# Hourglass attention and a gated FFN on one core: from pair 14 on, two head pairs share a stretch of scores and a stretch of outputs

## The chip, the cores and the metric

The kernel runs on one NeuronCore of a Trainium2 chip. The metric is the time of one execution in microseconds (us), as the device takes it; lower is better. The engines are named as in the profile: PE (TensorE, matrix products), PEld (its weight loads), DVE (VectorE), ACT (ScalarE), POOL (GpSimd) and SP (SyncE, which here issues DMAs only). Each works through its own instructions in order and waits for others by semaphores.

## What is computed

Attention over q, k, v of shape 8 x 8 x 576 x 64 (batch, head, position, width) in two parts that are added, and then a feed-forward network over the result:

```python
q_d, k_d, v_d = (t.reshape(B, H, 144, 4, D).mean(axis=3) for t in (q, k, v))
out_d = sm_attn(q_d, k_d, v_d)                    # softmax over all 144 pooled positions
out_up = np.repeat(out_d, 4, axis=2)
mask = np.abs(pos[:, None] - pos[None, :]) < 4    # a band of 7 keys a query
out_local = softmax(where(mask, scale * q @ k.T, -1e9)) @ v
x = (out_up + out_local).transpose(0, 2, 1, 3).reshape(4608, 512)
out = (np.maximum(x @ w_gate, 0) * (x @ w_val)) @ w_out   # 512 -> 1536 -> 512
```

## The kernel before, in words

**Attention** goes by pairs of heads: 32 pairs, pair `p` being heads 2p and 2p+1, four pairs to a batch. Per pair there are a pooled part (144 x 144 scores a head) and a local part (24 groups of 24 queries, each against 32 keys). On TensorE a pair needs five kinds of product: `pooled_v` (L352, v averaged over four positions), `pooled_out` (L367), `pooled_scores` (L382), `local_scores` (L407, 48 small ones) and `local_out` (L424, 48 small ones). Each kind addresses the array in tiles of its own shape, the profile's 128*32, 64*72, 64*32 and 32*64. Their results lie in two PSUM tensors of two banks each, `ata` and `atb`, at the column offsets `U, SCO, OD, VD1 = 0, 144, 336, 432` (L344). The other four banks, `fpsum`, rotate among the FFN's results.

**The other engines' part of a pair** is:

- ACT: `cast_q` and half of `cast_k` (L235, to fp16), `pooled_bias` (L447), four `pooled_exp` (L475), `local_exp` (L485), and the copies out of PSUM `evict_vd` (L489, L491) and `evict_od` (L546).
- DVE: `pooled_max` (L437), `add_mask` (L452), `local_max` (L460), the other half of `cast_k` (L237), `add_x` (L557, two instructions, adds both parts into `xT`), `pooled_recip` (L498), `local_sum` (L528, L529), `turn_local` (L540).
- POOL: `local_sub` (L463), `pool_q` and `pool_k` (L320 to L333, the sums over four positions of q and k into the tile `pd`, which `pooled_scores` reads), `pooled_weights` (L502), `local_weights` (L532), `cast_v` (L239).
- SP: the loads of q, k and v, the stores of y, and two DMAs that transpose: `turn_dma` (L314, casted q and k into `qkT`, from pair 11 on) and `turn_pooled` (L507, the pooled weights into `adT`).

**The FFN** goes by units in a fixed list. An `h` unit is 8 products of 512 columns (L573, the two halves of 128 hidden rows for 512 tokens), a relu on ACT (L582) and a product on DVE (L585, called the gate below); a `y` unit is 12 products (L598) and a copy on ACT (L607). A chunk of 512 tokens is 12 `h` and 4 `y` units. Its first `h` unit reads `xT` rows of four pairs, one pair for each of the four accumulated products.

**The order** of all instructions is that of the source; nothing reorders them. Pairs 0 to 8 and the first 11 FFN units go by the hand-written list `ORDER`. Then comes a loop over steps `s` from 9 to 33, which this change is about. A step starts the scores of pair `s` and the outputs of pair `s - 2` in one stretch on TensorE, and then puts one FFN unit at a time between the pieces of the other engines' work (L720 to L777). In each step from 14 on the four units are `h`, `y`, `h`, `h`. `store_y` issues the stores of finished y. After the loop 33 units of FFN alone are left.

Small tiles rotate by pair number: `pd` and `qkT` by 3, `vw`, `vd16`, `pT`, `adT` and `st32` by 4, `vst` by 3, `qk16`, `e_d`, `col`, `sm`, `dd`, `ee`, `pp`, `odx` by 2.

Of the kernel before, what the change touches and what calls it, by code (L numbers as in the profile page):

```python
# [14 lines left out]
AX = mybir.AxisListType  # L15

N_PE = 11
NEG = -1.0e9


# [73 lines left out]
def kernel(  # L94
# [201 lines left out]
    def flat(p):  # L296
        return qkT[p % 3].rearrange("p j t -> p (j t)")
# [43 lines left out]

    U, SCO, OD, VD1 = 0, 144, 336, 432  # L344

    def pooled_v(p, part=(0, 1)):
        for n in range(6):
            x = n % 4
            if n // 4 not in part:
                continue  # L350
            for h in range(2) if n >= 4 else (None,):
                nc.tensor.matmul(  # L352
                    out=atb[32 * x : 32 * x + 32, 1, OD : OD + 128]
                    if h is None
                    else ata[32 * x : 32 * x + 32, h, VD1 : VD1 + 64],
                    lhsT=p32,
                    rhs=vw[p % 4][:, :, n, :] if h is None else vw[p % 4][:, h, n, :],
                    start=True,
                    stop=True,
                    tile_position=(0, 32 * x),  # L360
                )

    def pooled_out(p):
        vd, ad = vd16[p % 4], adT[p % 4]
        for kc in range(2):
            for x in range(4):
                nc.tensor.matmul(  # L367
                    out=atb[32 * x : 32 * x + 32, 0, OD : OD + SD],
                    lhsT=vd[:, kc, 32 * x : 32 * x + 32],
                    rhs=ad[:, x // 2, :, kc, 0:72],  # L370
                    start=(kc == 0),
                    stop=(kc == 1),
                    tile_position=(0, 32 * x),
                    skip_group_check=True,
                )

    def pooled_scores(p):
        pdt = pd[p % 3]
        for c in range(2):
            for h in range(2):  # L380
                lo = 64 * h
                nc.tensor.matmul(  # L382
                    out=ata[0:72, h, SCO + SD * c : SCO + SD * c + SD],
                    lhsT=pdt[lo : lo + 64, c, 0, :],
                    rhs=pdt[lo : lo + 64, :, 1, :],
                    start=True,
                    stop=True,
                    tile_position=(lo, 0),
                )

    def local_scores(p):
        qt, kt = flat(p), k_view(qkT[p % 3])
        for n in range(6):
            for g in range(4):
                c, m = n // 3, 4 * (n % 3) + g
                b = 24 * (4 * n + g)
                for h in range(2):
                    lo = 64 * h
                    if p < N_PE:
                        queries = qt[lo : lo + 64, b + 584 * c : b + 584 * c + 32]  # L400
                        keys = qt[lo : lo + 64, S // 2 + b : S // 2 + b + 32]
                    else:
                        queries = qt[lo : lo + 64, b : b + 32]
                        keys = kt[lo : lo + 64, c, :, 6 * m : 6 * m + 8].rearrange(
                            "p r g -> p g r"
                        )
                    nc.tensor.matmul(  # L407
                        out=atb[32 * g : 32 * g + 32, h, SCO + 32 * n : SCO + 32 * n + 32],
                        lhsT=queries,
                        rhs=keys,  # L410
                        start=True,
                        stop=True,
                        tile_position=(lo, 32 * g),
                    )

    def scores(p):
        pooled_scores(p)
        local_scores(p)

    def local_out(p):  # L420
        for n in range(6):
            for h in range(2):
                for g in range(4):
                    nc.tensor.matmul(  # L424
                        out=(ata, atb)[g // 2][64 * h : 64 * h + 64, g % 2, U + 24 * n : U + 24 * n + 24],
                        lhsT=vw[p % 4][32 * g : 32 * g + 32, h, n, :],
                        rhs=pT[p % 4][32 * g : 32 * g + 32, 6 * h + n, 0:24],
                        start=True,
                        stop=True,
                        tile_position=(32 * g, 64 * h),  # L430
                    )
# [2 lines left out]

    def pooled_max(p):
        c = col[p % 2]
        nc.vector.tensor_reduce(  # L437
            out=c[0:72, 36:40].rearrange("p (h c) -> p h c", h=2),
            in_=ata[0:72, :, SCO : SCO + 2 * SD].rearrange("p h (c j) -> p h c j", c=2),
            axis=AX.X,  # L440
            op=ALU.max,
            negate=True,
        )
# [5 lines left out]
        )  # L449

    def add_mask(p):
        nc.vector.tensor_tensor(  # L452
            out=sm[p % 2].rearrange("p (h n) j -> p h (n j)", h=2),
            in0=atb[:, :, SCO : SCO + 192],
            in1=_sap(mask, (0, 128), 0, [[0, 2], [1, 192]]),
            op=ALU.add,
        )
# [11 lines left out]

    def pooled_exp(p, h):  # L470
        c = col[p % 2]
        for cc in range(2):
            hc = 2 * h + cc
            lo = SCO + SD * cc
            nc.scalar.activation(  # L475
                out=e_d[p % 2][0:72, h, cc, 0:6, 0:24],
                in_=ata[0:72, h, lo : lo + SD].rearrange("p (n j) -> p n j", j=24),
                func=AF.Exp,
                bias=c[0:72, 40 + hc : 41 + hc],
                scale=scale / 16.0,  # L480
                accum_out=c[0:72, 44 + hc : 45 + hc],
            )
# [3 lines left out]

    def evict_vd(p, kc):
        if kc == 0:
            nc.scalar.copy(out=vd16[p % 4][:, 0, :], in_=atb[:, 1, OD : OD + 128])  # L489
        else:  # L490
            nc.scalar.copy(  # L491
                out=vd16[p % 4][0:64, 1, :].rearrange("p (h d) -> p h d", h=2),
                in_=ata[0:64, :, VD1 : VD1 + 64],
            )

    def pooled_recip(p):
# [47 lines left out]
    def evict_od(p):  # L544

        nc.scalar.copy(  # L546
            out=odx[p % 2].rearrange("p (g n m) -> p g n m", g=4, n=6),
            in_=atb[:, 0, OD : OD + SD].rearrange("p (n g m) -> p g n m", g=4, n=6),
        )

    def add_x(p, half=(1, 0)):
        b, kk = p // 4, p % 4
        x = xT[:, kk, b * S : (b + 1) * S].rearrange(
            "p (n g m f) -> p g n m f", n=6, g=4, f=4
        )
        for i in half:
            nc.vector.tensor_tensor(  # L557
                out=x[:, 2 * i : 2 * i + 2],
                in0=(ata, atb)[i][:, :, U : U + SD].rearrange(
                    "p g (n m f) -> p g n m f", n=6, f=4  # L560
                ),
                in1=_sap(odx[p % 2], (0, 128), 72 * i, [[36, 2], [6, 6], [1, 6], [0, 4]]),
                op=ALU.add,
            )
# [152 lines left out]
        stages[stage](int(number), *engine)  # L717
    pos[0] = ORDER.count("ga:")

    for s in range(9, NP + 2):  # L720
        now, nxt, two = s < NP, s + 1 < NP, s + 2 < NP
        if s + 3 < NP:
            load_qk(s + 3)
            load_v(s + 3)
        store_y()
        if now:
            pooled_v(s)
        pooled_out(s - 2)
        if now:
            scores(s)  # L730
        local_out(s - 2)
        evict_od(s - 2)
        if nxt:
            cast_v(s + 1, "pool")
        if now:
            evict_vd(s, 0)
            pooled_max(s)
            add_mask(s)
            local_max(s)
            local_sub(s)  # L740
        if two:
            cast_q(s + 2, "act")
        ffn(1)
        if now:
            pooled_bias(s)
            pooled_exp(s, 0)
            pooled_exp(s, 1)
        if two:
            cast_k(s + 2, 0, "dve")
        add_x(s - 2)  # L750
        if nxt and s + 1 >= N_PE:
            pool_q(s + 1)
            pool_k(s + 1)
        if now:
            local_exp(s)
            evict_vd(s, 1)
            pooled_recip(s)
            pooled_weights(s)
            local_sum(s)
            local_weights(s)  # L760
        ffn(1)
        if two:
            cast_k(s + 2, 1, "act")
            turn_dma(s + 2)
        if now:
            turn_pooled(s)
        if s + 1 < N_PE:
            turn_pe(s + 1)
            evict_half(s + 1, 0, None, "act")
# [2 lines left out]
            evict_half(s + 1, 1, 1, "dve")  # L772
            evict_sums(s + 1, 1, "dve")
        ffn(1)
        if now:
            turn_local(s)
        ffn(1)  # L777
    while pos[0] < len(units):
        ffn(1)
        store_y()  # L780
# [30 lines left out]
```

## Time and profile before

| what | us |
|---|---|
| runs of the kernel | 383.83, 388.38, 388.03; median 388.03 |
| the profiled execution | 384.85 |
| its span, first to last instruction | 383.1 |
| PE busy / DVE / ACT / POOL in the span | 362.6 / 217.0 / 214.2 / 183.1 |
| one step of the loop at 210 to 220 us | 9.50 |

In the rows of the timeline the first number is the start in us from the span's start, the second how long it took; x counts instructions merged into the row, and in brackets stand idle time ahead of it and what ended it. An instruction of DVE, ACT or POOL can start some hundredths before the record of the one ahead of it ends, so what an instruction costs its engine is read from start to start. A PE row's length holds the time to pass the array, so TensorE too is read from start to start.

### The profile page before, as it was taken

To read this page: it belongs to the slowest core of one execution; us is meant where nothing else is said; L and a number is where in the kernel's file an instruction comes from. 1 tells how busy PE (TensorE), PEld (TensorE's weight loads), DVE (VectorE), ACT (ScalarE), POOL (GpSimd) and SP (SyncE) were. 2 spreads that over 40 slices of the span, in tenths; PEclk is the share of its full clock that TensorE was granted. 3 is DMA by queue.
4 is the path that set the end of the run, shared out by engine and by line. 5 is a ranking of instruction groups with operands and counts; after the bars stand their busy time and mean duration, and the time that the engine had idled before them with its cause. 6 is when DMAs were issued, how large, how long until landed. Compare 5 with 4: busy or idle time off the path is not lost.

```text
span 383.1 us, 13146 instructions
## 1 busy us (share of the span) xinstructions
PE 362.6 (95%) x5476; PEld 186.1 (49%) x5476; DVE 217.0 (57%) x456; ACT 214.2 (56%) x644; POOL 183.1 (48%) x242
## 2 busy tenths in 40 slices
PE   2877997899999999999999999999999999999996
PEld 2756543454554444455545554555554444444442
DVE  2766785566666666666666666666666232222220
ACT  3868685366666666666666666666655322333231
POOL 5788785435666666666666666666652000000000
PEclk9955699899999999999999999999999999999999
DMA  7998999968889999999999999995842000100012
GB/s 263 257 239 247 193 205 207 207 115 173 191 189 190 190 190 193 185 196 182 200 190 187 194 174 202 197 190 119 153 68 70 29 29 29 55 27 29 27 40 99
DMA packets 140920, 58.63 MB, mean 153 GB/s; under 512 B 121852, under 2 KB 133308, under 8 KB 140860
## 3 DMA queue, kind: packets, MB, share of 16 engines
q1 hardware_dynamic: 135660, 52.93, 65.7%
q0 software_dynamic: 4768, 4.72, 7.7%
q8 instruction: 43, 0.70, 0.8%
q10 hardware_dynamic: 432, 0.14, 0.2%
q14 instruction: 17, 0.14, 0.1%
HBM read 42.05 MB, written 9.44 MB: 134 GB/s over the span
## 4 chain that ended last, share of the span: by engine, by line
PE 85%; DMA 5%; POOL 3%; SPq 2%; issue 2%; DVE 1%; ACT 1%; POOLq 0%; ACTq 0%; DVEq 0%
PE h_ps L573 47%; PE y_ps L598 24%; DMA vst<-in_v_dram 5%; PE atb L407 3%; PE ata L424 3%; PE ata L382 2%; PE t_ps L286 2%; PE atb L424 1%; SPq L177 1%; PE atb L367 1%; PE atb L352 1%; PE t_ps L280 1%; SPq L218 1%; POOL dd L463 1%; POOL qk L239 1%
## 5 line engine op out<-in xcount | busy, mean ns | idle before, releaser
L585 DVE TENSOR_TENSOR gT<-r,h_ps 128x512 f16<-128x512 f16 x108 | 74.0, 686 | 97.4 <-PE h_ps L573 92.6
L573 PE MATMUL h_ps<-xT,wg 128*128 128x512 f16 x432 | 113.2, 386 | 0.0
L573 PE MATMUL h_ps<-xT,wv 128*128 128x512 f16 x432 | 111.1, 381 | 0.0
L598 PE MATMUL y_ps<-wo,gT 128*128 128x512 f16 x432 | 98.6, 379 | 0.0
L582 ACT ACTIVATE r<-h_ps 128x512 f16<-128x512 f32 x108 | 64.3, 597 | 49.9 <-PE h_ps L573 49.8
L463 POOL TENSOR_TENSOR dd<-sm,col 128x384 f32<-128x384 f32 x32 | 26.6, 832 | 86.0 <-DVE col L460 86.0
L598 PEld LDWEIGHTS <-gT 128*128 128x128 f16 x432 | 42.3, 98 | 50.9
L573 PEld LDWEIGHTS <-wv 128*128 128x128 f16 x432 | 42.1, 98 | 50.7 <-issue 1.1
L573 PEld LDWEIGHTS <-wg 128*128 128x128 f16 x432 | 39.9, 99 | 45.3 <-issue 2.0
L475 ACT ACTIVATE e_d<-ata,col 72x144 f16<-72x144 f32 x128 | 46.7, 370 | 1.4 <-PE ata L352 0.2
L607 ACT COPY y_sb<-y_ps 128x512 f32<-128x512 f32 x36 | 21.1, 586 | 40.0 <-PE y_ps L598 39.8
L502 POOL TENSOR_TENSOR e_d<-e_d,col 72x576 f16<-72x576 f16 x32 | 36.6, 1144 | 4.8 <-DVE col L498 3.5
L437 DVE TENSOR_REDUCE col<-ata 72x4 f32<-72x576 f32 x32 | 24.1, 753 | 23.5 <-PE atb L424 21.2
L546 ACT CAST odx<-atb 128x144 f16<-128x144 f32 x32 | 8.9, 279 | 49.5 <-PE atb L424 47.6
L235 ACT CAST qk<-st 96x768 f16<-96x768 f32 (+3 forms) x45 | 33.5, 745 | 1.6 <-DMA st<-in_k_dram 1.6
L239 POOL CAST vw<-vst 128x768 f16<-128x768 f32 x32 | 26.3, 823 | 7.9 <-DMA vst<-in_v_dram 5.0
L532 POOL TENSOR_TENSOR pp<-ee,col 128x384 f16<-128x384 f16 x32 | 26.5, 831 | 0.0
L475 ACT ACTIVATION_READ_ACCUMULATOR e_d<-ata,col 72x1 f32 x128 | 24.9, 194 | 0.0
L540 DVE STREAM_TRANSPOSE pT<-pp 128x384 f16<-128x384 f16 x32 | 18.3, 573 | 9.2 <-POOL pp L532 9.1
L424 PE MATMUL atb<-pT,vw 32*64 32x24 f16 x768 | 18.7, 190 | 1.8 <-issue 1.8
L452 DVE TENSOR_TENSOR sm<-atb,mask 128x384 f32<-128x384 f32 x32 | 17.5, 545 | 2.8 <-POOL vw L239 1.0
L407 PE MATMUL atb<-qkT 64*32 64x32 f16 x1536 | 18.3, 211 | 0.7 <-issue 0.7
(52 smaller groups left out, 378.0 us busy)
## 6 DMA issues: line engine op xcount, KB each, us to landing
vst<-in_v_dram SPq DMA_DIRECT2D x126, 96.0 KB, 4.7
st<-in_q_dram SPq DMA_DIRECT2D x32, 288.0 KB, 4.8
out_dram<-y_sb SPq DMA_DIRECT2D x36, 256.0 KB, 3.3
st<-in_k_dram SPq DMA_DIRECT2D x20, 320.0 KB, 6.0
st<-in_k_dram SPq DMA_DIRECT2D x11, 288.0 KB, 5.0
wo<-in_moe_w_out_dram POOLq DMA_DIRECT2D x4, 384.0 KB, 7.8
wg<-in_moe_w_gate_dram POOLq DMA_DIRECT2D x2, 384.0 KB, 6.5
wv<-in_moe_w_val_dram POOLq DMA_DIRECT2D x2, 384.0 KB, 7.3
```

Of the source, the lines that this page charges most:

```text
L235: nc.scalar.copy(out=out, in_=in_)
L239: nc.gpsimd.tensor_copy(out=out, in_=in_)
L407: nc.tensor.matmul(out=atb[32 * g : 32 * g + 32, h, SCO + 32 * n : SCO + 32 * n + 32], lhsT=queries, rhs=keys, start=True, stop=True, tile ...
L424: nc.tensor.matmul(out=(ata, atb)[g // 2][64 * h : 64 * h + 64, g % 2, U + 24 * n : U + 24 * n + 24], lhsT=vw[p % 4][32 * g : 32 * g + 32, ...
L463: nc.gpsimd.tensor_tensor(out=dd[p % 2], in0=sm[p % 2], in1=_sap(col[p % 2], (0, 128), 0, [[1, 12], [0, 32]]), op=ALU.subtract,)
L475: nc.scalar.activation(out=e_d[p % 2][0:72, h, cc, 0:6, 0:24], in_=ata[0:72, h, lo : lo + SD].rearrange("p (n j) -> p n j", j=24), func=AF ...
L502: nc.gpsimd.tensor_tensor(out=ed, in0=ed, in1=_sap(col[p % 2], (0, 72), 48, [[1, 4], [0, 6], [0, 24]]), op=ALU.mult)
L532: nc.gpsimd.tensor_tensor(out=pp[p % 2], in0=ee[p % 2], in1=_sap(col[p % 2], (0, 128), 24, [[1, 12], [0, 32]]), op=ALU.mult,)
L573: nc.tensor.matmul(out=ps, lhsT=(wg, wv)[i][:, kk, 128 * j : 128 * j + 128], rhs=xT[:, kk, TCH * c : TCH * c + TCH], start=(kk == 0), stop ...
L582: nc.scalar.activation(out=r1[j % 3], in_=h_ps[c, j, 0], func=AF.Relu)
L585: nc.vector.tensor_tensor(out=gT[c % 2][:, j, :], in0=r1[j % 3], in1=h_ps[c, j, 1], op=ALU.mult)
L598: nc.tensor.matmul(out=ps, lhsT=gT[c % 2][:, j, 128 * t : 128 * t + 128], rhs=wo[:, j, :], start=(j == 0), stop=(j == NJ - 1),)
```

## The change

Steps 9 to 13 stay single steps. From pair 14 (`TWO`) on, one pass of a loop handles an even pair `e` and the odd pair `o = e + 1`. It has two stretches on TensorE: the first with the scores of both pairs, the second with `pooled_v` of both and the outputs of the two pairs before (`e - 2`, `o - 2`). Four FFN units stand behind each stretch, so the number of FFN units per pair is as before.

The columns of PSUM are laid out anew. All scores of an even pair lie in `ata`, all of an odd pair in `atb`. The results of the second stretch lie in columns that held scores in the first: `pooled_v`, `pooled_out` and `local_out` of both pairs side by side.

```diff
+    def lay(p):
+        if p < TWO:
+            return ata, 144, atb, 144
+        t = (ata, atb)[p % 2]
+        return t, 0, t, 288
+    def lay_vd(p):
+        if p < TWO:
+            return atb[:, 1, 336 : 336 + 128], ata[:, :, 432 : 432 + 64]
+        if p % 2:
+            return atb[:, 1, 288 : 288 + 128], atb[:, :, 416 : 416 + 64]
+        return atb[:, 0, 288 : 288 + 128], ata[:, :, 432 : 432 + 64]
+    def lay_out(p):
+        if p < TWO - 2:
+            return 0, atb[:, 0, 336 : 336 + SD]
+        return SD * (p % 2), ata[:, p % 2, 288 : 288 + SD]
```

Steps 9 to 13 keep their order, but both `cast_q` and the DVE half of `cast_k` now stand ahead of the first FFN unit, and three of these steps prepare one pair more (for each step: the pairs to load, to cast and turn, to pool):

```diff
+    ahead = {s: ((s + 3,), (s + 2,), (s + 1,)) for s in range(9, 11)}
+    ahead[11] = (14, 15), (13,), (12,)
+    ahead[12] = (16,), (14, 15), (13,)
+    ahead[13] = (17,), (16,), (14, 15)
```

The new loop (`ready_turn(p, 0)` is `cast_q` on ACT and half of `cast_k` on DVE; `ready_turn(p, 1)` is the other half on ACT and `turn_dma`; `ready_pool` is `pool_q` and `pool_k`; `load(p, pv)` is `load_qk(p)`, `load_v(pv)` and `store_y`; `pooled_chain` is `pooled_recip` and `pooled_weights`; `local_chain` is `local_exp`, `local_sum` and `local_weights`):

```diff
+    for e in range(TWO, NP + 2, 2):
+        o = e + 1
+        now = e < NP
+        load(e + 4, e + 3)
+        if now:
+            pooled_scores(e)
+            pooled_scores(o)
+            local_scores(e)
+            local_scores(o)
+            pooled_max(e)
+            add_mask(e)
+            pooled_max(o)
+            cast_v(o, "pool")
+        ffn(1)
+        if now:
+            add_mask(o)
+            local_max(e)
+            local_sub(e)
+            pooled_bias(e)
+            pooled_exp(e, 0)
+            pooled_exp(e, 1)
+        ffn(1)
+        if now:
+            local_max(o)
+            pooled_bias(o)
+            pooled_exp(o, 0)
+            pooled_exp(o, 1)
+            local_sub(o)
+            pooled_chain(e)
+        ffn(1)
+        if now:
+            local_chain(e)
+        ready_turn(e + 3, 0)
+        ready_pool(e + 2)
+        ffn(1)
+        ready_turn(e + 3, 1)
+        if now:
+            turn_pooled(e)
+            turn_local(e)
+        load(e + 5, e + 4)
+        if now:
+            pooled_v(e)
+            pooled_v(o)
+        pooled_out(e - 2)
+        pooled_out(o - 2)
+        local_out(e - 2)
+        local_out(o - 2)
+        evict_od(e - 2)
+        evict_od(o - 2)
+        if now:
+            evict_vd(e, 0)
+            evict_vd(o, 0)
+            evict_vd(o, 1)
+            evict_vd(e, 1)
+        if e + 2 < NP:
+            cast_v(e + 2, "pool")
+        ffn(1)
+        add_x(e - 2)
+        add_x(o - 2)
+        if now:
+            local_exp(o)
+            pooled_chain(o)
+            local_sum(o)
+            local_weights(o)
+        ffn(1)
+        ready_turn(e + 4, 0)
+        ready_pool(e + 3)
+        ffn(1)
+        ready_turn(e + 4, 1)
+        if now:
+            turn_pooled(o)
+        ffn(1)
+        if now:
+            turn_local(o)
```

The last pass, e = 32, has no scores, only the outputs of pairs 30 and 31.

More of the change, by code (lines that the diff above doesn't have):

```diff
@@ L17 @@
 N_PE = 11
+TWO = 14
 NEG = -1.0e9
@@ L338, in pool_k @@
         )
-    U, SCO, OD, VD1 = 0, 144, 336, 432
+    def lay(p):
[13 more added lines that the diff above has]
+        return SD * (p % 2), ata[:, p % 2, 288 : 288 + SD]
     def pooled_v(p, part=(0, 1)):
+        vd0, vd1 = lay_vd(p)
         for n in range(6):
@@ L352, in pooled_v @@
                 nc.tensor.matmul(
-                    out=atb[32 * x : 32 * x + 32, 1, OD : OD + 128]
-                    if h is None
-                    else ata[32 * x : 32 * x + 32, h, VD1 : VD1 + 64],
+                    out=(vd0 if h is None else vd1[:, h])[32 * x : 32 * x + 32, :],
                     lhsT=p32,
@@ L367, in pooled_out @@
                 nc.tensor.matmul(
-                    out=atb[32 * x : 32 * x + 32, 0, OD : OD + SD],
+                    out=lay_out(p)[1][32 * x : 32 * x + 32, :],
                     lhsT=vd[:, kc, 32 * x : 32 * x + 32],
@@ L378, in pooled_scores @@
         pdt = pd[p % 3]
+        t, col0 = lay(p)[:2]
         for c in range(2):
@@ L382, in pooled_scores @@
                 nc.tensor.matmul(
-                    out=ata[0:72, h, SCO + SD * c : SCO + SD * c + SD],
+                    out=t[0:72, h, col0 + SD * c : col0 + SD * c + SD],
                     lhsT=pdt[lo : lo + 64, c, 0, :],
@@ L392, in local_scores @@
         qt, kt = flat(p), k_view(qkT[p % 3])
+        t, col0 = lay(p)[2:]
         for n in range(6):
@@ L407, in local_scores @@
                     nc.tensor.matmul(
-                        out=atb[32 * g : 32 * g + 32, h, SCO + 32 * n : SCO + 32 * n + 32],
+                        out=t[32 * g : 32 * g + 32, h, col0 + 32 * n : col0 + 32 * n + 32],
                         lhsT=queries,
@@ L420, in local_out @@
     def local_out(p):
+        u = lay_out(p)[0]
         for n in range(6):
@@ L424, in local_out @@
                     nc.tensor.matmul(
-                        out=(ata, atb)[g // 2][64 * h : 64 * h + 64, g % 2, U + 24 * n : U + 24 * n + 24],
+                        out=(ata, atb)[g // 2][64 * h : 64 * h + 64, g % 2, u + 24 * n : u + 24 * n + 24],
                         lhsT=vw[p % 4][32 * g : 32 * g + 32, h, n, :],
@@ L436, in pooled_max @@
         c = col[p % 2]
+        t, col0 = lay(p)[:2]
         nc.vector.tensor_reduce(
             out=c[0:72, 36:40].rearrange("p (h c) -> p h c", h=2),
-            in_=ata[0:72, :, SCO : SCO + 2 * SD].rearrange("p h (c j) -> p h c j", c=2),
+            in_=t[0:72, :, col0 : col0 + 2 * SD].rearrange("p h (c j) -> p h c j", c=2),
             axis=AX.X,
@@ L451, in add_mask @@
     def add_mask(p):
+        t, col0 = lay(p)[2:]
         nc.vector.tensor_tensor(
             out=sm[p % 2].rearrange("p (h n) j -> p h (n j)", h=2),
-            in0=atb[:, :, SCO : SCO + 192],
+            in0=t[:, :, col0 : col0 + 192],
             in1=_sap(mask, (0, 128), 0, [[0, 2], [1, 192]]),
@@ L471, in pooled_exp @@
         c = col[p % 2]
+        t, col0 = lay(p)[:2]
         for cc in range(2):
             hc = 2 * h + cc
-            lo = SCO + SD * cc
+            lo = col0 + SD * cc
             nc.scalar.activation(
                 out=e_d[p % 2][0:72, h, cc, 0:6, 0:24],
-                in_=ata[0:72, h, lo : lo + SD].rearrange("p (n j) -> p n j", j=24),
+                in_=t[0:72, h, lo : lo + SD].rearrange("p (n j) -> p n j", j=24),
                 func=AF.Exp,
@@ L488, in evict_vd @@
         if kc == 0:
-            nc.scalar.copy(out=vd16[p % 4][:, 0, :], in_=atb[:, 1, OD : OD + 128])
+            nc.scalar.copy(out=vd16[p % 4][:, 0, :], in_=lay_vd(p)[0])
         else:
@@ L492, in evict_vd @@
                 out=vd16[p % 4][0:64, 1, :].rearrange("p (h d) -> p h d", h=2),
-                in_=ata[0:64, :, VD1 : VD1 + 64],
+                in_=lay_vd(p)[1][0:64],
             )
@@ L547, in evict_od @@
             out=odx[p % 2].rearrange("p (g n m) -> p g n m", g=4, n=6),
-            in_=atb[:, 0, OD : OD + SD].rearrange("p (n g m) -> p g n m", g=4, n=6),
+            in_=lay_out(p)[1].rearrange("p (n g m) -> p g n m", g=4, n=6),
         )
@@ L552, in add_x @@
         b, kk = p // 4, p % 4
+        u = lay_out(p)[0]
         x = xT[:, kk, b * S : (b + 1) * S].rearrange(
@@ L558, in add_x @@
                 out=x[:, 2 * i : 2 * i + 2],
-                in0=(ata, atb)[i][:, :, U : U + SD].rearrange(
+                in0=(ata, atb)[i][:, :, u : u + SD].rearrange(
                     "p g (n m f) -> p g n m f", n=6, f=4
@@ L718, with pooled_chain, local_chain @@
     pos[0] = ORDER.count("ga:")
[L720 to L724, printed above, removed]
+    ahead = {s: ((s + 3,), (s + 2,), (s + 1,)) for s in range(9, 11)}
+    ahead[11] = (14, 15), (13,), (12,)
+    ahead[12] = (16,), (14, 15), (13,)
+    ahead[13] = (17,), (16,), (14, 15)
+    def pooled_chain(p):
+        pooled_recip(p)
+        pooled_weights(p)
+    def local_chain(p):
+        local_exp(p)
+        local_sum(p)
+        local_weights(p)
@@ L725 @@
+    for s in range(9, TWO):
+        to_load, to_turn, to_pool = ahead[s]
+        for p in to_load:
+            load_qk(p)
+        load_v(s + 3)
         store_y()
-        if now:
-            pooled_v(s)
+        pooled_v(s)
         pooled_out(s - 2)
-        if now:
-            scores(s)
+        scores(s)
         local_out(s - 2)
         evict_od(s - 2)
[L733 to L740, printed above, removed]
@@ L741 @@
-        if two:
-            cast_q(s + 2, "act")
-        ffn(1)
[L744 to L749, printed above, removed]
-        add_x(s - 2)
[L751 to L760, printed above, removed]
@@ L761 @@
-        ffn(1)
[L762 to L766, printed above, removed]
+        cast_v(s + 1, "pool")
+        evict_vd(s, 0)
+        pooled_max(s)
+        add_mask(s)
+        local_max(s)
+        local_sub(s)
+        for p in to_turn:
+            cast_q(p, "act")
+            cast_k(p, 0, "dve")
+            if p != to_turn[-1]:
+                cast_k(p, 1, "act")
+                turn_dma(p)
+        ffn(1)
+        pooled_bias(s)
@@ L767 @@
+        pooled_exp(s, 0)
+        pooled_exp(s, 1)
+        add_x(s - 2)
+        for p in to_pool:
+            if p >= N_PE:
+                pool_q(p)
+                pool_k(p)
+        local_exp(s)
+        evict_vd(s, 1)
+        pooled_chain(s)
+        local_sum(s)
+        local_weights(s)
+        ffn(1)
+        cast_k(to_turn[-1], 1, "act")
+        turn_dma(to_turn[-1])
+        turn_pooled(s)
         if s + 1 < N_PE:
@@ L774, with load, ready_turn, ready_pool @@
         ffn(1)
-        if now:
-            turn_local(s)
-        ffn(1)
+        turn_local(s)
+        ffn(1)
+    def load(p, pv):
+        if p < NP:
+            load_qk(p)
+        if pv < NP:
+            load_v(pv)
+        store_y()
+    def ready_turn(p, step):
+        if p >= NP:
+            return
+        if step == 0:
+            cast_q(p, "act")
+            cast_k(p, 0, "dve")
+        else:
+            cast_k(p, 1, "act")
+            turn_dma(p)
+    def ready_pool(p):
+        if p < NP:
+            pool_q(p)
+            pool_k(p)
```

## The prediction

> **What bounds the kernel now.** I read the page's busy shares and slices first, then a table of stretches, then the timeline of one step, engine by engine.
>
> ```profile
> PE 362.6 (95%) x5476; PEld 186.1 (49%) x5476; DVE 217.0 (57%) x456; ACT 214.2 (56%) x644; POOL 183.1 (48%) x242
> PE   2877997899999999999999999999999999999996
> POOL 5788785435666666666666666666652000000000
> 172.00:210.00 38.00, 38.00 (x609) 19.10 (x608) 25.68 (x53) 24.67 (x77) 23.61 (x33) 1.00 0.96 190
> 210.30:219.80 9.50, 9.50 (x153) 4.77 (x152) 6.42 (x14) 6.17 (x19) 5.90 (x9) 1.00 1.01 195
> ```
>
> From slice 8 on PE is full; in the table of stretches (length, then busy time of PE, PEld, DVE, ACT, POOL) it works all 38.00 of 38 us. The waits of PE from 170 to 295 us are an empty list. So TensorE sets the end, and only two things move it: less time on TensorE, or a new wait of TensorE. One step of TensorE:
>
> ```profile
> 209.37 1.03 PE L573 MATMUL h_ps<-xT,wv 128*128 128x512 f16 x4
> 210.32 0.24 PE L352 MATMUL atb<-vw,p32c 128*32 128x128 f16 x4
> 210.67 0.32 PE L382 MATMUL ata<-pd 64*72 64x144 f16 x4
> 210.92 0.58 PE L407 MATMUL atb<-qkT 64*32 64x32 f16 x48
> 211.96 1.04 PE L573 MATMUL h_ps<-xT,wg 128*128 128x512 f16 x4
> ```
>
> Four products of 512 columns stand 0.863 us apart (208.50 to 209.37), 0.2157 each. So the FFN ends at 210.23, and the pair's stretch lasts to 211.96: 1.73 us. An h unit is 1.73, a y unit 2.59, the step's four units 7.77.
>
> POOL, one step, and an exception further on:
>
> ```profile
> 213.98 0.83 POOL L463 TENSOR_TENSOR dd<-sm,col 128x384 f32<-128x384 f32 x1 [3.44 <-DVE col L460]
> 214.76 0.85 POOL L320 TENSOR_TENSOR ptq<-qkT 128x288 f32<-128x288 f16 x1
> 216.89 0.49 POOL L333 TENSOR_TENSOR pd<-ptk 128x144 f16<-128x144 f32 x1
> 217.34 1.14 POOL L502 TENSOR_TENSOR e_d<-e_d,col 72x576 f16<-72x576 f16 x1
> 218.44 0.83 POOL L532 TENSOR_TENSOR pp<-ee,col 128x384 f16<-128x384 f16 x1
> 219.22 0.82 POOL L239 CAST vw<-vst 128x768 f16<-128x768 f32 x1
> 272.62 0.67 POOL L320 TENSOR_TENSOR ptq<-qkT 128x288 f32<-128x288 f16 x1 [0.75 <-DMA qkT<-qk]
> ```
>
> The next pair's pooled q and k (L320 to L333) run here ahead of L502 and L532 and are done at 217.38; `pooled_scores` reads them at 220.18, 2.8 us later. That is the cover the change touches. And DVE, whose rows the new chain needs:
>
> ```profile
> 215.50 0.46 DVE L557 TENSOR_TENSOR xT<-ata,odx 128x288 f16<-128x288 f32 x1
> 215.88 0.16 DVE L498 RECIPROCAL col<-col 72x4 f32<-72x4 f32 x1
> 218.28 0.69 DVE L585 TENSOR_TENSOR gT<-r,h_ps 128x512 f16<-128x512 f16 x1 [1.54 <-PE h_ps L573]
> ```
>
> **Part 1, time on TensorE.** Instruction counts stay. What goes is changes of tile shape. Reading starts singly: into the stretch 210.23 to 210.325, 0.09; L367 to L382 (last start 210.516, 144 columns 0.06) 0.10; L382 to L407 0.09; L407 to L424 (211.285 to 211.426, less 0.01) 0.13; out 0.12. Ten such gaps for two pairs, 1.06 us. After: in, L382 to L407, out; in, L367 to L424, out: 0.09+0.09+0.12 and 0.09+0.13+0.12 = 0.64. So 0.42 is saved per pass (bounds 0.3 to 0.5, the unseen L407-to-FFN and L367-to-L424 gaps lying between 0.09 and 0.13). Nine passes: -3.7. The last pass puts two stretches of 0.80 (pairs 30, 31) into one: -0.3. Together **-4.0**.
>
> **Part 2, the new wait.** `ready_pool(e + 3)` pools the odd pair of the next pass. It now stands behind `pooled_weights(o)` and `local_weights(o)` on POOL, and these behind unit 5's gate and four `add_x` on DVE. Its reader, `pooled_scores(o + 2)`, opens the next pass. Time from the first product of unit 5 (h), which follows the second stretch:
>
> - gate starts 2.00 (unit start 216.28, gate 218.28), costs 0.61 (213.96 to 214.57): 2.61;
> - four `add_x` at 0.38 (215.50 to 215.88): 4.13. At 215.01 to 215.50 one cost 0.49, held by ACT's reads of `ata`; ACT's copies are done by then, so 0.38;
> - reciprocal 0.16, to POOL 0.09 (213.89 to 213.98): 4.38;
> - L502 1.10 (217.34 to 218.44): 5.48; L532 0.78 (218.44 to 219.22): 6.26;
> - L320 to the end of L333: 2.62 (214.76 to 217.38), or 2.43 where L320 took 0.67 (272.62 to 275.05): 8.69 to 8.88;
> - to PE 0.06 (a cast ended 17.80, PE started 17.85): 8.75 to 8.94.
>
> TensorE would come to that product after units h, y, h, h, 7.77, the gap 0.09 and `pooled_scores(e + 2)` 0.15 (210.67 to 210.825): 8.01. It waits 0.74 to 0.93; I take the middle, 0.84. The long L320 lies beside a `cast_k` on DVE (214.57 to 215.09), the short one beside none; in the new place none is beside L320, but one falls beside L502, so both ends stay. The Trainium skill's "SBUF — State Buffer" (Who interferes with whom) says that a DVE cast in a two-port mode and GpSimd lock each other out, while a DVE instruction with one SBUF input does not. These rows agree; by that rule alone the wait would be the short end, 0.74, and the sum 0.8 lower.
>
> TensorE runs in order, so local scores and FFN queue behind the wait, and each pass starts the chain anew: nothing catches up. It happens at the start of passes 16 to 30, eight times (pair 15 is pooled in step 13, and pass 32 has no scores): 8 x 0.84 = **+6.7**, bounds 5.9 to 7.4.
>
> **Part 3, what costs nothing, and why.** `add_x(o - 2)` ends near 4.2; its reader, the fourth product of unit 7 at a chunk's start, comes at 4.32+0.65. The casts turn in the first half: ACT ends `cast_k(e + 3)` near the second stretch's end, the transpose takes 3.7 to 4.7 us to land, and POOL wants it at 6.26: 1.5 to spare. SP waits there, with `turn_pooled(e)` and seven DMAs of the mid-pass `load` queued behind; their readers are ten us or more off. `cast_v(e + 2)` ends on POOL at 3.6, before the 4.38. The FFN's four banks come free over 0.7 us ahead of their next use. Steps 11 to 13: the earlier `cast_k` delays gates by 0.45, which have a unit's time; step 12 casts two pairs ahead of a relu, 1.3 us late, covered the same way; step 13 pools two pairs on POOL, done 7.9 after its stretch, wanted at 8.0: 0 to +0.5, taken as 0.
>
> Second stretch: it needs ACT's reads of the odd pair's scores done. From the first stretch's end: relu 1.06, bias 0.24, exps 1.44, copy of y at 4.52 and 0.49, bias 0.24, exps 1.44 and tail: 6.8. TensorE arrives at 7.77+0.09. 1.0 to spare.
>
> **Sum.** -4.0 + 6.7 = **+2.7 us**. On the profiled execution: 384.85 + 2.7 = 387.6 (span 385.8). That execution lies 3.2 below the median 388.03; the four known times are 383.83, 384.85, 388.03, 388.38, mean 386.3. From there: **389**.
>
> **Rivals.**
>
> *B, no wait.* The chain of part 2 is 0.8 short of what I add up, or the wait hides. For it: POOL is busy 0.59 of a step and had 2.8 us to spare. Against: every link is a row, in order on two engines. Then only part 1 is left: 386.3 - 4.0 = 382.
>
> *C, slower by over 2%.* The odd pair's exps write `e_d`, which `turn_pooled(o - 2)` of the pass before still reads. SP issues it at about 8.3 (behind the `turn_dma` at 6.9), it lands at most 5.0 later (median 3.3 in the loop), at 13.3, and ACT wants the tile 5.25 after the next first stretch, at 15.3. If it lands over 2.0 later still, the exps are late, and 1.0 more brings TensorE to a stop at the second stretch, eight times. It decides from a landing of 8.0 us instead of 5.0; with 0.65 more than that per pass the time is over 394. For it: the DMA share is already 0.96 to 1.01, and two transposes now stand right behind seven loads. Against: no landing in the loop's list is over 6.2. A page has a rule that makes C sharper. The row first: at 281.82 `add_x` on `ata` waited 0.31 us for ACT's exp, though they read other columns. The Trainium skill's "PSUM — Partial Sum Buffer" (PSUM bank collisions raise a hardware error) says to guard by bank and quadrant, not by address, and the row agrees. By that rule disjoint columns free nothing: the second stretch waits for the last exp at 6.8; by columns alone its first products could start after `add_mask(o)` at 3.2, and C would be nearly shut.
>
> **How the numbers follow.** My forecast (a wait of 0.5 to 1.3 at the odd pair's pooled scores, 386.3 to 392.7): 0.56. B: 0.20. C, or the wait of part 2 at over 1.4 us for another reason: 0.24. The range reaches from B's 382 to early C, **382 to 396**; the forecast's own is 385 to 393. Over 2% is 7.7 us here, about what a measurement of this kernel can tell from no change. Faster by that needs twice part 1: 0.03. Slower needs (7.7+4.0)/8 = 1.46 us a pass: 0.23, nearly all of C. Within: 0.74.
>
> **What would show it.** Right: the waits of PE list eight of about 0.8 us at L382, released by POOL's `pd` (L333), 19.4 us apart from about 145 us on (pass 16); a first stretch near 1.4 us without its wait, the second near 1.6; L382-to-L424 gaps gone. POOL goes L502, L532, L320 without idle time in the second half. Wrong: no such wait, period 18.6 us (B); PE waiting at L352 for ACT's L475, and ACT for a DMA ahead of that (C); or a stretch no shorter than two old ones, which would undo part 1.

## The result, and the profile after

| | us, median (lowest to highest) | runs |
|---|---|---|
| before | 387.45 (383.79 to 389.6) | 14 |
| after | 392.76 (388.84 to 394.64) | 14 |
| ratio | 1.0142, 95% interval 1.0097 to 1.0188 | |

The change costs 5.5 us (3.8 to 7.3). The profiled execution after took 394.62 us, span 392.9; it lies at the slow end of its runs. Of the 9.8 us that its span is over that of before, 1.4 arose ahead of step 9, where the source is the same, and 1.7 do not come from the change either: the granted clock was 0.72 between 79.3 and 85.4 us, where before had 1.00, and the FFN units of step 9 ahead of TensorE's own transposes took 6.01 us instead of 4.33. Two executions of one kernel, e7 and e10 below, have 6.01 and 4.33 there. So costs below are read from the loop, and the totals from the ratios.

The page after, busy times and POOL's slices:

```profile
PE 361.7 (92%) x5476; PEld 185.2 (47%) x5476; DVE 219.6 (56%) x456; ACT 210.7 (54%) x644; POOL 180.8 (46%) x242
POOL 5796679334646675747474838383553000000000
```

PE has the same instructions, and its busy time is even 0.9 us less. What grew is the time between them. POOL, even before, now alternates 7 and 4, 8 and 3: its work piles up in the second half of each pass. What PE waited for from 130 to 300 us (total, times, longest), where before had an empty list:

```profile
PE atb L406 <- POOL pd L334: 4.0, 7, 0.7
PE atb L377 <- ACT e_d L504: 2.0, 1, 2.0
```

The new line numbers: pooled scores L406 (was L382), local scores L432 (L407), `pooled_v` L377 (L352), local outputs L450 (L424), FFN products L603 and L628, pooled weights L531, local weights L561, pooled q and k L321 to L334, exps L504.

I measure a stretch from the end of the last FFN product (its start plus 0.216) to the start of the next. Passes 16 to 24 of the profile are alike to 0.01 us:

| | first stretch | second | FFN, four units |
|---|---|---|---|
| two steps before | 1.72 | 1.72 | 7.78 |
| pass 14 | 1.40 | 1.58 | 7.78 |
| passes 16 to 24 | 2.15 | 1.58 | 7.78 |
| pass 26 | 2.39 | 1.58 | 7.78 |
| pass 28 | 2.15 | **3.60** | **9.47** after the second |
| pass 30 | 1.72 | 1.55 | 7.78 |
| step 12 (before the loop) | 1.67 | | **9.41** |

The table adds up to the other 6.7 us of the span: shorter stretches take 4.4 us away, eight waits at the first stretch add 5.8 (0.75 in most, 0.99 in pass 26, 0.32 in pass 30), step 12 adds 1.6 and pass 28 adds 3.7.

The first stretch of pass 20 with its wait, and then the chain of the same pass, on DVE and on POOL, that ends in the wait of pass 22:

```profile
186.59 0.32 PE L406 MATMUL ata<-pd 64*72 64x144 f16 x4
187.47 0.32 PE L406 MATMUL atb<-pd 64*72 64x144 f16 x4 [0.56 <-POOL pd L334]
```
```profile
200.02 0.69 DVE L615 TENSOR_TENSOR gT<-r,h_ps 128x512 f16<-128x512 f16 x1 [1.01 <-PE h_ps L603]
202.09 0.16 DVE L527 RECIPROCAL col<-col 72x4 f32<-72x4 f32 x1
202.86 2.30 DVE L238 CAST qk<-st 74x512 f16<-74x512 f32 x1
```
```profile
202.33 1.14 POOL L531 TENSOR_TENSOR e_d<-e_d,col 72x576 f16<-72x576 f16 x1 [0.78 <-DVE col L527]
203.43 0.83 POOL L561 TENSOR_TENSOR pp<-ee,col 128x384 f16<-128x384 f16 x1
204.22 0.66 POOL L321 TENSOR_TENSOR ptq<-qkT 128x288 f32<-128x288 f16 x1
206.22 0.49 POOL L334 TENSOR_TENSOR pd<-ptk 128x144 f16<-128x144 f32 x1
```

Unit 5 starts at 198.01. Gate at 2.01, reciprocal at 4.08, L531 at 4.32, `pd` complete at 206.71, 8.70: the prediction had 2.00, 4.13, 4.38 and 8.69 to 8.88. In its new place L321 takes 0.66, the short one of the two known values. The wait list shows 0.6 of the 0.75, since idle time is counted from the modelled end of the product ahead.

Two places nearly alike are new. **Step 12**: SP, ACT and PE of the profile after.

```profile
101.60 1.42 SPq L183 DMA_DIRECT2D st<-in_q_dram  x1
104.14 3.43 SPq L219 DMA_DIRECT2D vst<-in_v_dram  x4
108.57 2.26 SPq L315 DMA_TRANSPOSE qkT<-qk  x1
```
```profile
114.72 0.83 ACT L236 CAST qk<-st 96x768 f16<-96x768 f32 x1 [2.38 <-DMA qkT<-qk]
```
```profile
116.10 1.02 PE L603 MATMUL h_ps<-xT,wv 128*128 128x512 f16 x4 [0.26 <-ACT r L612]
119.04 1.02 PE L603 MATMUL h_ps<-xT,wv 128*128 128x512 f16 x4 [1.05 <-ACT y_sb L637]
```

Step 11 loads q and k of two pairs. SP comes to the transpose of pair 13 at 108.57, and it lands near 114.7. The cast of pair 15 writes the buffer that this transpose reads, so ACT stands still ahead of a relu, and TensorE runs out of free FFN banks: 1.63 us.

**Pass 28**: the same engines.

```profile
261.37 4.03 SPq L196 DMA_DIRECT2D st<-in_k_dram  x2
265.45 3.40 SPq L219 DMA_DIRECT2D vst<-in_v_dram  x4
269.53 1.45 SPq L315 DMA_TRANSPOSE qkT<-qk  x1
271.03 1.80 SPq L536 DMA_TRANSPOSE adT<-e_d  x1
```
```profile
274.35 0.38 ACT L504 ACTIVATE e_d<-atb,col 72x144 f16<-72x144 f32 x1 [3.10 <-DMA adT<-e_d]
```
```profile
275.95 0.24 PE L377 MATMUL atb<-vw,p32c 128*32 128x128 f16 x4 [1.96 <-ACT e_d L504]
```

The last piece of pair 31's k (L196) shares rows 57 to 63 with the piece ahead of it and waits for that to land; SP stands there. The transpose of pair 27's weights is issued at 271.03 for that reason, ACT's exps of pair 29 wait for it, and TensorE's second stretch waits for the exps: 2.0 us. The units behind take 1.7 us more for another reason: TensorE is busy all the time there, but at a granted clock of 0.82 (a stretch and its length, then busy times of PE, PEld, DVE, ACT and POOL, granted clock, DMA share, GB/s):

```profile
277.40:286.90 9.50, 9.50 (x48) 3.88 (x36) 5.45 (x14) 4.78 (x14) 7.50 (x12) 0.82 0.51 113
```

In the twelve traces of this case such a drop of the clock stands, between 100 and 300 us, at five of the twelve single stops of TensorE of more than 1.4 us (here, in e3 and e4, twice in e5) and nowhere else. That the stop brings it about is likely, but no run shows it. Before, SP stood at the same two DMAs for 4.95 us, and nothing that was due was queued behind.

### The profile page after: what moved, and what is told of

Its sections match the earlier page's. It is cut to its first block, busy times and chain, and to the rows that moved or that the text cites. A ratio compares the mean times of both kernels' runs of the same rounds, so it can differ in the third digit from the quotient of the medians.

```text
span 392.9 us, 13165 instructions
## 1 busy us (share of the span) xinstructions
PE 361.7 (92%) x5476; PEld 185.2 (47%) x5476; DVE 219.6 (56%) x456; ACT 210.7 (54%) x644; POOL 180.8 (46%) x242
## 5 line engine op out<-in xcount | busy, mean ns | idle before, releaser
L603 PE MATMUL h_ps<-xT,wg 128*128 128x512 f16 x432 | 114.3, 388 | 1.3 <-issue 1.3
L603 PE MATMUL h_ps<-xT,wv 128*128 128x512 f16 x432 | 112.4, 384 | 1.3 <-ACT y_sb L637 1.1
L628 PE MATMUL y_ps<-wo,gT 128*128 128x512 f16 x432 | 99.5, 381 | 0.0
L603 PEld LDWEIGHTS <-wv 128*128 128x128 f16 x432 | 42.3, 99 | 53.0 <-issue 4.1
L628 PEld LDWEIGHTS <-gT 128*128 128x128 f16 x432 | 42.6, 99 | 52.3 <-issue 2.2
L603 PEld LDWEIGHTS <-wg 128*128 128x128 f16 x432 | 40.0, 99 | 47.5 <-issue 3.4
L531 POOL TENSOR_TENSOR e_d<-e_d,col 72x576 f16<-72x576 f16 x32 | 36.6, 1143 | 17.9 <-DVE col L527 14.9
L561 POOL TENSOR_TENSOR pp<-ee,col 128x384 f16<-128x384 f16 x32 | 26.7, 835 | 26.7 <-DVE col L558 25.1
L504 ACT ACTIVATE e_d<-ata,col 72x144 f16<-72x144 f32 x92 | 33.5, 370 | 1.8 <-DVE sm L480 0.3
L238 DVE CAST qk<-st 74x512 f16<-74x512 f32 (+1 forms) x22 | 21.3, 968 | 6.4 <-DMA st<-in_k_dram 4.4
L464 DVE TENSOR_REDUCE col<-ata 72x4 f32<-72x576 f32 x23 | 17.3, 751 | 11.0 <-PE atb L450 4.5
L450 PE MATMUL atb<-pT,vw 32*64 32x24 f16 x768 | 16.6, 190 | 3.8 <-issue 3.8
L504 ACT ACTIVATION_READ_ACCUMULATOR e_d<-ata,col 72x1 f32 x92 | 18.0, 196 | 0.0
L450 PEld LDWEIGHTS <-vw 32*64 32x64 f16 x1536 | 14.7, 107 | 6.3 <-issue 4.4
L587 DVE TENSOR_TENSOR xT<-ata,odx 128x288 f16<-128x288 f32 x32 | 14.4, 450 | 5.2 <-PE atb L450 3.0
```

The costliest lines, as they stand in the source:

```text
L238: nc.vector.tensor_copy(out=out, in_=in_)
L450: nc.tensor.matmul(out=(ata, atb)[g // 2][64 * h : 64 * h + 64, g % 2, u + 24 * n : u + 24 * n + 24], lhsT=vw[p % 4][32 * g : 32 * g + 32, ...
L504: nc.scalar.activation(out=e_d[p % 2][0:72, h, cc, 0:6, 0:24], in_=t[0:72, h, lo : lo + SD].rearrange("p (n j) -> p n j", j=24), func=AF.E ...
L531: nc.gpsimd.tensor_tensor(out=ed, in0=ed, in1=_sap(col[p % 2], (0, 72), 48, [[1, 4], [0, 6], [0, 24]]), op=ALU.mult)
L561: nc.gpsimd.tensor_tensor(out=pp[p % 2], in0=ee[p % 2], in1=_sap(col[p % 2], (0, 128), 24, [[1, 12], [0, 32]]), op=ALU.mult,)
L603: nc.tensor.matmul(out=ps, lhsT=(wg, wv)[i][:, kk, 128 * j : 128 * j + 128], rhs=xT[:, kk, TCH * c : TCH * c + TCH], start=(kk == 0), stop ...
```

## The experiments

Theory P: the POOL chain makes the wait of 0.75. Theory S: late issues on SP make the two other losses. Rivals stand with each run. Ratios are to the kernel before; their intervals are 0.003 to 0.008 wide to either side, so what a single edit does is read from its trace.

| run | ratio | 95% interval |
|---|---|---|
| e1_rows_disjoint | 1.0083 | 1.0041 to 1.0124 |
| e2_load15_sooner | 1.0136 | 1.0075 to 1.0197 |
| e3_recip_first | 1.0100 | 1.0053 to 1.0147 |
| e4_scores_by_turns | 1.0102 | 1.0023 to 1.0180 |
| e5_cast_v_in_chain | one time, 395.2 us | |
| e6_all_three | 0.9962 | 0.9922 to 1.0002 |
| e7_all_and_e_d3 | 0.9890 | 0.9820 to 0.9960 |
| e8_e_d3_alone | 1.0080 | 1.0041 to 1.0118 |
| e9_pool_chain_left | 1.0035 | 1.0006 to 1.0064 |
| e10_best_again | 0.9903 | 0.9870 to 0.9937 |

**The wait, link by link.**

```diff
+        if now:
+            pooled_recip(o)
         add_x(e - 2)
         add_x(o - 2)
         if now:
             local_exp(o)
-            pooled_chain(o)
+            pooled_weights(o)
```

> Only DVE's reciprocal of the odd pair's pooled sums moves, ahead of the four add_x. Theory P (the chain gate, add_x, reciprocal, POOL L531, L561, L321 to L334 ends last at the odd pair's pooled scores): POOL starts L531 when its cast of v is done, 3.5 us after unit 5 starts instead of 4.3, and the wait of 0.75 us at the first stretch nearly goes (under 0.1) in passes 16 to 30: 5 to 6 us less, 0.999 to 1.001 of the kernel before. Rival T (the transposed q and k of the odd pair arrive last, and POOL's earlier work is only in their shadow): POOL waits for the DMA instead, and the wait stays over 0.5 us, the time at 1.012 to 1.014.

Four first stretches fall from 2.15 to 1.75, the others lie at 1.80 to 2.14 (pass 30 at 1.40). Up to 1.50 was expected; 2.6 of the 5.8 us go, and the time, 1.0100, misses the 0.999 to 1.001. POOL of that run says why:

```profile
157.94 1.14 POOL L531 TENSOR_TENSOR e_d<-e_d,col 72x576 f16<-72x576 f16 x1
159.44 0.83 POOL L561 TENSOR_TENSOR pp<-ee,col 128x384 f16<-128x384 f16 x1 [0.36 <-DVE col L558]
```

L531 starts as soon as the cast of v ends, but L561 needs the local sums, which still stand behind `add_x` on DVE. The next link took over at 0.36. POOL has no wait for a DMA between 130 and 300 us of that run, so rival T falls.

```diff
-        if e + 2 < NP:
-            cast_v(e + 2, "pool")
         ffn(1)
 ...
             local_weights(o)
+        if e + 2 < NP:
+            cast_v(e + 2, "pool")
```

> POOL's cast of v for the next even pair moves from the idle time ahead of the chain to a place inside it, behind the odd pair's local weights. Theory P: the chain gets 0.80 us longer, and the wait at the odd pair's pooled scores goes from 0.75 to about 1.55 us: first stretches of passes 16 to 28 take 2.95 us instead of 2.15, pass 14 stays at 1.40; 5.6 to 6.4 us more in all. Rival T (a DMA or another engine ends the wait, POOL is only near): the stretches stay at 2.15.

First stretches of 2.92 us in most passes, pass 14 still 1.40. Its waits of PE:

```profile
PE atb L406 <- POOL pd L334: 11.1, 8, 1.8
```

A cast of 0.82 put into the chain lengthens the wait by 0.77. POOL ends it. The FFN units behind two of these waits, in passes 18 and 26, take 9.5 us instead of 7.78, at a granted clock of 0.82.

**The price of a change of tile shape.**

```diff
             pooled_scores(e)
-            pooled_scores(o)
             local_scores(e)
+            pooled_scores(o)
             local_scores(o)
```

> The first stretch goes pooled e, local e, pooled o, local o instead of pooled e, pooled o, local e, local o: two changes of tile shape more, and the odd pair's pooled scores start 0.5 us later. Theory P with part 1's price of a change (0.09 to 0.13): the local scores of e cover 0.5 us of the wait, which falls from 0.75 to about 0.15, and two changes add 0.2: the first stretch takes 1.75 us instead of 2.15, 0.4 less in seven passes, 2 to 3 us in all, 1.007 of the kernel before; pass 14, which has no wait, shows the two changes alone, 1.40 to 1.6. Rival F (a change of shape costs next to nothing between short products): pass 14 stays at 1.40 and the others fall to 1.55.

Pass 14, without a wait, takes 1.60 us. That alone would not do, since with the first order it takes 1.40 to 1.54 in the traces, by gaps among its last local scores. Read from starts, the two added changes cost 0.09 (L406 to L432) and 0.13 (L432 to L406). Rival F falls. Four of the other passes take 1.72 to 1.74, the rest 1.66 to 2.32. The wait is a deadline: work put ahead of it comes out of the wait. The next limit shows at once:

```profile
PE atb L377 <- ACT e_d L504: 2.5, 2, 2.0
PE atb L406 <- POOL pd L334: 1.2, 3, 0.6
```

**Pass 28 and step 12.**

```diff
-            for lo, n in ((0, 64), (57, 16)):
+            for lo, n in ((0, 64), (64, 9)):
```

> The last two pieces of pair 31's k are loaded without common rows (0 to 63 and 64 to 72 instead of 0 to 63 and 57 to 72). Theory S (SP's queue): the second piece waited for the first to land, with the transposed weights of pair 27 queued behind it, so ACT's exps of pair 29 and TensorE's second stretch of pass 28 came late. Then the 3 us between the two issues go, the second stretch of pass 28 shrinks from 3.60 to about 1.6 us and the FFN behind it from 9.47 to 7.78: 3.7 us less in the trace, about 0.990 of the changed kernel, 1.005 of the kernel before. Rival N (DMA load at that moment, whatever the rows): the exps of pair 29 still wait for the transpose, and the time stays at 1.014.

SP's two DMAs take 1.10 us instead of 4.03, and the next transpose of weights is issued at 264.56; pass 28 takes 1.58 and 7.78 us, as the others. Theory S holds. The ratio falls by 0.006, not 0.010, though its interval holds the expected 1.005 too. The expectation took the profile's 3.7 us for every run's: the second stretch of this pass takes 3.05 in the trace of e2_load15_sooner, without the drop of the clock behind it, 3.17 in that of e3_recip_first and 4.01 in that of e4_scores_by_turns. And pass 30, to which the stop had given time, goes from 1.72 to 2.08.

```diff
-    e_d = many(2, [80, 2, 2, 8, 32], FP16, "e_d")
+    e_d = many(3, [80, 2, 2, 8, 32], FP16, "e_d")
```

(and `e_d[p % 3]` at its four uses)

> The changed kernel with e_d by three, nothing else. Theory C (pass 28's 3.7 us come through e_d: ACT may not write it until the transpose of pair 27 has read it): the second stretch of pass 28 takes 1.6 us instead of 3.60 and the FFN behind it 7.78, though the load of pair 31 still holds SP for 3 us; the seven waits of 0.75 stay; 3 to 3.7 us less, 1.005 of the kernel before. Rival V (something else that SP issues late, adT or v, is what ends the wait): pass 28 stays over 3 us and the time at 1.014.

SP and ACT of that run in pass 28:

```profile
258.12 4.03 SPq L196 DMA_DIRECT2D st<-in_k_dram  x2
267.23 1.69 SPq L536 DMA_TRANSPOSE adT<-e_d  x1
```
```profile
268.00 0.38 ACT L504 ACTIVATE e_d<-atb,col 72x144 f16<-72x144 f32 x1
```

SP is held as long as ever, but the exps start 0.8 us after the transpose is issued, without a wait, and the pass takes 1.58 and 7.78. So the path is SP, then the transpose, then `e_d`, then ACT, then TensorE; it is cut at either end.

```diff
-    ahead[11] = (14, 15), (13,), (12,)
+    ahead[10] = (13, 14), (12,), (11,)
+    ahead[11] = (15,), (13,), (12,)
```

> Pair 14's q and k are loaded in step 10 and pair 15's alone in step 11, instead of both in step 11. Theory S: in step 11 two pairs' loads held SP until 108.57, so the transpose of pair 13 was issued 2 us late and ACT's cast of pair 15, which writes the same buffer, waited 2.38 us ahead of a relu. Then that wait goes, and the FFN of step 12 takes 7.78 us instead of 9.41: 1.6 us less, about 1.010 of the kernel before. Rival A (ACT's own work of two pairs ahead of the relu is the cause): the two casts stay ahead of the relu, so the FFN of step 12 stays near 9.4 us and the time at 1.014.

The FFN of step 12 takes 8.12 us instead of 9.41, though ACT still casts two pairs ahead of the relu; its wait for the transpose falls from 2.38 to 0.96. In the six traces without this edit these units take 9.2 to 9.8 us, in the five with it 7.8 to 8.3; where the wait is gone altogether (e7, e9) they take 7.78, so the two casts alone cost nothing, and rival A falls. The ratio, 1.0136 from four runs, hardly moves, and its interval holds what either theory expected. The traces decide for S; the time alone is inconclusive.

**Together.** e6 is e1, e2 and e3, and in addition:

```diff
             local_sum(o)
-            local_weights(o)
         ffn(1)
         ready_turn(e + 4, 0)
         ready_pool(e + 3)
+        if now:
+            local_weights(o)
```

> The three repairs together, and the odd pair's local weights go behind the pooled q and k of the next odd pair on POOL, since with the reciprocal alone POOL waited 0.36 us for the local sums there. Theory P with S: first stretches 1.40 to 1.50 us, second 1.58, step 12 at 8.1, no wait in pass 28; against the kernel before 9 x 0.46 + 0.27 less and up to 0.4 + 0.6 more, 3.4 to 4.2 us, 0.989 to 0.991. Rival D (the transposes land later the sooner TensorE comes: the new limit is the DMA queue): waits appear at the second stretches of several passes, for ACT's exps, and the time is 0.995 to 1.005.

No longer slower than before (the interval just reaches 1), but less than part 1 gives. ACT's waits in the loop of that run, 130 to 300 us:

```profile
ACT e_d L504 <- DMA adT<-e_d: 4.1, 6, 1.1
```

With TensorE 0.75 us a pass sooner, the exps of the odd pair come up against the transpose in six passes. They delay the next relu, local sums and POOL, and first stretches are 1.40 to 1.72. Rival D was right in its size and in what ACT waits for. It was wrong in the place where TensorE waits and in the reason: after the change alone these exps start 4.4 to 5.0 us after the transpose is issued, without a wait (pass 28 apart); here the six that wait start 3.6 to 4.3 after it. The transposes are not later, the exps would come sooner.

> As the run before it, and e_d, which the transposes of the pooled weights read, rotates by three instead of two. Theory D of the run before (ACT's exps of the odd pair wait until the transpose of the odd pair before has read the tile): no wait of ACT for that DMA and none of TensorE's second stretch for ACT is left, 0.988 to 0.991 of the kernel before, less than e6_all_three by what its waits add up to. Theory P with S alone: no waits to take away, the same time as e6_all_three within 0.003.

The waits of PE from 130 to 300 us are an empty list again; all nine first stretches are 1.40, the second ones 1.58 (1.55 at the end), step 12 has 7.78. One pass of it:

```profile
202.12 0.32 PE L406 MATMUL ata<-pd 64*72 64x144 f16 x4
202.27 0.29 PE L406 MATMUL atb<-pd 64*72 64x144 f16 x4
```

Last, the wait by itself: e9 is e1, e2 and e_d by three, with the chain left as the change has it; e10 is e7 again.

> Everything of e7_all_and_e_d3 but the POOL order: sooner load, rows without overlap and e_d by three, with the odd pair's chain as in the changed kernel. Theory P: the wait at the odd pair's pooled scores is all that parts it from e7_all_and_e_d3: eight first stretches of 2.15 us instead of 1.40, 6.0 us, so 1.003 to 1.006 of the kernel before (-4.4 + 6.0 = +1.6 us). Rival R (waits left in the chain hide in other waits): below 0.998.

> e7_all_and_e_d3 once more on the same chip as the run beside it. Theory: an undisturbed loop, first stretches 1.40, second 1.58, 4.4 us less than the kernel before: 0.986 to 0.991. Rival: its earlier 0.989 owed something to the spread of the runs, and it lies within 0.994 to 1.002.

All that PE waits for in e9, 100 to 300 us:

```profile
PE atb L406 <- POOL pd L334: 4.4, 8, 0.6
```

Between the two lie 0.0132, 5.1 us by ratios; by the traces seven waits of 0.75 and one of 0.69, 5.9 us. e10 beats both kernels: 382.6 us median, 3.8 us (2.4 to 5.0) under before. Its trace has 1.40 in seven first stretches, 1.50 and 1.54 in two without a wait, and 8.28 in step 12.

## Why the prediction was right, and where it was short

It gave 389 and a range of 382 to 396; the median is 392.76. The direction and both named mechanisms came out, the sum was +2.7 us against +5.5. That the time still lies in the range is in part luck: the range was drawn wide for B and C, the forecast's own, 385 to 393, holds the time by 0.24 us, and most of the loss comes from two places that the sum had at nothing. 1.15 of the 3.8 us between 389 and the median are the base, 386.3 from four times, where 14 runs have 387.45.

- *Part 1, 0.42 us a pass saved*: 1.40 + 1.58 against 3.44 is 0.46; two changes of shape cost 0.09 and 0.13 (e4). The last pass saves 0.27 (0.3). In all 4.4 us against the 4.0 predicted, and with every wait gone the kernels e7 and e10 gain 4.3 and 3.8. (9 x 0.42 is 3.8, not 3.7.)
- *Part 2, a wait of 0.74 to 0.93, taken as 0.84*: 0.75, at the short end, since L321 ran in 0.66. Eight passes have it; pass 26 0.99, where L561 took 1.01 us instead of 0.83 and the last local scores 0.1 more; pass 30 less (0.32), as pass 28's stop had given POOL time (0.69 where that stop is gone, e9). The value taken was 0.09 too long. The cast that was to fall beside L502 alone lasted past L321 (last section), and L321 was still the short one.
- *Part 3, "Steps 11 to 13: ... covered the same way"*: wrong. It followed ACT's and DVE's work but put SP's queue at the pace of the steps before. Two pairs' loads in one step held SP until 108.57, and the transpose that frees the cast buffer came late: 1.63 us in step 12, costed at 0.
- *Rival C* was kept as a case of its own, deciding at a landing of 8.0 us. Its path was right (transpose, `e_d`, exps, second stretch), its trigger not. The landings that the trace gives stayed at 2.6 to 4.6 us (median 3.5, before 3.3); the issue was late. SP issued this one 10.7 us after unit 5's start (198.01), not 8.3:

```profile
208.76 1.21 SPq L536 DMA_TRANSPOSE adT<-e_d  x1
213.24 0.38 ACT L504 ACTIVATE e_d<-atb,col 72x144 f16<-72x144 f32 x1
```

From issue to exps there are 4.48 us, and it landed 4.36 after its issue: 0.12 to spare in this pass, 1.0 with the median, where the prediction had 2.0 with the longest landing. One DMA that waits for another, in the trace of before for 4.95 us and overlooked there, used that up in pass 28: 2.0 us of waiting, and 1.7 at the lower clock behind it.
- *Rival B* (no wait) fell, and the 1.46 us a pass that slower by over 2% needed were not reached. POOL's share of a step, given for B as 0.59, is 0.62 (5.90 of 9.50 us).

By ratios: the chain and part 1 together are +0.0035 (e9), about 1.4 us, where the prediction had +2.7; step 12 and pass 28 are the other 0.0107, about 4.1 us (by traces 1.6 and, less what pass 30 gains, 3.3), which it had at zero in the sum. The rule of the Trainium skill's "PSUM — Partial Sum Buffer" (PSUM bank collisions raise a hardware error), that disjoint columns of a bank free nothing, fits how the program's semaphores guard the banks, and the trace shows no more than that: in pass 28 `pooled_v` of the even pair (L377) writes columns 288 to 415 of `atb`, whose earlier reader `add_mask(o)` was done at 269.21, and yet waited until 275.95 for the exps, which read columns 0 to 287.

## What to carry to other kernels

When work of two steps is batched, the engine that was the bound gains what the sum of its gaps says (0.46 us a pass here), but each producer now has one deadline where it had two; list for every consumer at the head of the batch what stands ahead of its producer on the producer's own queue. Do that for the DMA queue as well: a transpose queued behind loads is late by their issue times, and by any wait inside them. When a wait is removed, the next one is often already there (0.36 us in e3, six waits of ACT in e6), so look at the idle times of the whole chain before counting the gain.

## What the runs showed of the hardware that was not expected

In six of seven passes DVE's cast of k took 2.30 us (202.86) beside POOL's L531, L561 and L321, and 0.36 (197.34) where POOL was mostly idle. The Trainium skill's "SBUF — State Buffer" (Who interferes with whom) says that a DVE cast in a two-port mode and a GpSimd instruction lock each other out for a whole instruction. The trace does not tell the cast's mode, but fits that: the cast ended 0.28 us after the third of POOL's in a row, L321, at 204.88. It delayed the next gate by some 0.8 us (205.09, where 2.0 after the unit's start would be 204.33), and TensorE did not wait for that. The issue of the loads on SP took unequal times too: four loads of v took 3.43 us in step 11, behind the loads of q and k of two pairs, and 2.00 in step 12, behind those of one.
